# Attention with a gated dense block: head 0 one query tile at a time, its keys transposed on TensorE, wo loaded later

## The chip, the cores, the metric

One core of one Trainium2 chip. The metric is the device time of one execution, in microseconds (us). In the profile lines PE is TensorE, PEld its weight loads, DVE is VectorE, ACT is ScalarE, POOL is GpSimd and SP is SyncE, whose queue issues most of the loads.

## The reference, cut to what matters

```python
xn = _layernorm(x)                                   # x: 2048 x 512
q  = (xn @ wq) -> 32 heads of 128                    # wq: 512 x 4096
scores = einsum(q, k_cache) * 128 ** -0.5            # 2048 keys per head
o  = softmax(scores) @ v_cache                       # per head
s  = o @ wo                                          # wo: 4096 x 512
h  = relu(xn @ w1 + b1) ** 2                         # w1: 512 x 1792
g  = silu(h @ w2 + b2)
return x + s * g
```

## The kernel before: the parts that matter

Queries come in 4 blocks of 512, each with 32 heads: 128 pairs of block and head, called heads 0 to 127. A head has 8 steps of two key tiles (128 keys each); step pi belongs to head pi // 8. In each step TensorE does two score matmuls of 512 columns, up to three *fillers*, and eight PV matmuls for the step two earlier. ScalarE does one exponential of 1024 columns. Fillers are everything else TensorE has to do: later heads' projections, the dense block, wo. PV is the product of the exponentials with the values. In PSUM, psA holds scores, psO the PV sums, psF what fillers make; NPR is 8, LAG is 2.

```python
for pi in range(NPAIR):                      # 1024 steps
    g, k = divmod(pi, NPR)
    gen_scores(pi)                           # waits: exp of pi-2, keys, queries of head g
    ...
    most = 0 if pi == 0 else 4 if pi == 1 else 3 if k == 2 else 2
    while n < most:                          # fillers, paced by a credit (work left / steps left)
        ...
        fill_one(pi)
    if pi >= LAG:
        gen_pv(pi - LAG)                     # waits: exp of pi-2
```

Fillers alternate between two PSUM banks. A job fills one bank with its matmuls, VectorE copies it out, and the job after next needs that bank again:

```python
    (n, mm, evac), i = cur[0]
    bank = bank_no[0]
    mm(i, bank)                              # waits for t_bankF[bank]
    if i == n - 1:
        t_bankF[bank] = evac(bank, step)     # the VectorE copy that frees it
        bank_no[0] ^= 1
```

Head 0 starts cold. Before, all four query tiles of the first block were normalised, transposed and projected; the keys came by a DMA transpose; then the eight steps ran as for any head:

```python
    fill_k(0)                                # DMA transpose, 512 KB
    ...                                      # statistics and scales of 4 tiles
    warm_up(15)                              # dummy matmuls, for the clock
    first_transpose(0); warm_up(3); first_transpose(1); ...
    first_proj(0); first_transpose(2); ...; first_proj(3)
    first_evac(3, 1, DV)
    t_evac[0] = t_bankF[1]                   # the first score waits for this
```

The softmax here doesn't subtract the row's maximum and nothing guards it: scores larger than these inputs give would overflow.

Of the kernel before, what the change touches and what calls it, by code (L numbers as in the profile page):

```python
# [6 lines left out]
ALU = mybir.AluOpType  # L7
# [207 lines left out]
def bass_recurrent_scan__mha_block_cached__dense_activation_squared_relu__prompt_kernel(  # L215
# [84 lines left out]
    psO = nc.alloc_psum_tensor("psO", [P, 2, 2, 256], F32)  # L300
# [4 lines left out]

    sl_k = [S.slot(f"k{i}") for i in range(NSL)]
    sl_v = [S.slot(f"v{i}") for i in range(NSL)]
    sl_wq = [S.slot(f"wq{i}") for i in range(NSW)]
# [34 lines left out]
    def ln_stats(j, i):  # L343
        jt = j * TPB + i
        prev = [t_xn.get(jt - TPB), t_xr.get(jt - TPB)]
        t = E(DV, partial(_bn_stats, out=st_t[:, i, :], in_=x_ln[:, i, :]),
              deps=[t_xl[jt]] + prev)
        t = E(DV, partial(_bn_aggr, out=mv_t[:, i, :], in_=st_t[:, i, :]), deps=[t])
# [4 lines left out]
                                 op=ALU.pow), deps=[t, t_mhalf])  # L353

# [17 lines left out]
    def first_scale(i):  # L372

        t = E(GP, partial(_tt, out=nm_t[:, i:i + 1], in0=mv_t[:, i, 0:1], in1=rstd[:, i:i + 1],
                          op=ALU.mult), deps=[t_xr[i]])
        t = E(GP, partial(_ts, out=nm_t[:, i:i + 1], in0=nm_t[:, i:i + 1], scalar1=-1.0,
                          scalar2=0.0, op0=ALU.mult, op1=ALU.add), deps=[t])
        t_xn[i] = E(AC, partial(_act, out=xn_t[:, i, :], in_=x_ln[:, i, :], func=ACT.Identity,
                                scale=rstd[:, i:i + 1], bias=nm_t[:, i:i + 1]), deps=[t])

    def first_view(i):
        return psA[:, i * 512:i * 512 + 256].bitcast(BF16)

    def first_transpose(i):
        for c in range(NDC):
            t = E(PE, partial(_peT, out=first_view(i)[:, c * P:(c + 1) * P],
                              in_=xn_t[:, i, c * P:(c + 1) * P], ident=ident[:]),
                  deps=[t_xn[i], t_ident], inc=(c == NDC - 1))
        t_xnr[i] = t

    def first_copy(i, eng):
        out, in_ = xnT[:, :, i * P:(i + 1) * P], first_view(i).rearrange("p (c q) -> p c q", q=P)
        op = (partial(_act, out=out, in_=in_, func=ACT.Copy) if eng is AC
              else partial(_copy, out=out, in_=in_))
        tok_xT[0][i] = E(eng, op, deps=[t_xnr[i]])

    def first_proj(i):
        for c in range(NDC):
            t = E(PE, partial(_mm, out=bankF(i // 3)[:, i * P:(i + 1) * P], lhsT=wq_sb[:, 0, c, :],
                              rhs=xnT[:, c, i * P:(i + 1) * P], start=(c == 0),  # L400
                              stop=(c == NDC - 1)),
                  deps=[t_wqfill[0], tok_xT[0][i]], inc=(c == NDC - 1))
        t_proj[0] = t

    def first_evac(i, n, eng):
        out, in_ = qt_sb[:, 0, i * P:(i + n) * P], bankF(i // 3)[:, i * P:(i + n) * P]
        op = (partial(_act, out=out, in_=in_, func=ACT.Copy) if eng is AC
              else partial(_copy, out=out, in_=in_))
        t_bankF[i // 3] = E(eng, op, deps=[t_proj[0]])

    def warm_up(n):
        for _ in range(n):
            E(PE, partial(_mm, out=bankF(1), lhsT=warm[:, 0:P], rhs=warm[:], start=True,
                          stop=True), deps=[t_warm], inc=False)
# [18 lines left out]
    def fill_k(g):  # L433
        if g >= NG:
# [3 lines left out]
                                sl_k[i], deps=[t_S_last[prev] if prev >= 0 else None])  # L438
# [25 lines left out]
    def gen_scores(pi):  # L464
# [4 lines left out]
        for n in range(2):  # L469
            tt = 2 * k + n  # L470
# [343 lines left out]
    for i in range(TPB):  # L814
        ln_stats(0, i)
        if i < 2:
            first_scale(i)
# [124 lines left out]
```

## Time and profile before

| | before |
|---|---|
| time, median of the first 3 runs | 1241.44 us (1240.85 to 1241.76) |
| span in the trace | 1238.3 us |
| TensorE busy / ScalarE busy | 1232.8 / 1057.3 us |
| first score of head 0 starts | 10.75 us |

Busy time of TensorE counts the latency of single matmuls (379 ns on average at 512 columns, though they start 216 ns apart) and the warm-ups, so it says only that there is hardly a gap. Where it works and where it only looks busy has to be read from starts. The prediction shows the lines.

### The profile page before, as it was taken

Reading aid. Unit: us, or ns where it says so; the run is one execution under the profiler, and the core shown is the slowest. Engines: PE = TensorE matmul, PEld = TensorE weight load, DVE = VectorE, ACT = ScalarE, POOL = GpSimd, SP = SyncE. Lnnn points to the kernel's source line nnn. Section 1 sums busy time; section 2 is a strip of 40 time slices with the busy share of each in tenths; the row PEclk is TensorE's granted clock in tenths of the full one; section 3 lists DMA queues with packets and bytes.
Section 4 is the critical chain, followed back from the end, with each engine's and each line's share of the span. In section 5 each row is a group of like instructions: output and inputs, shape, how many; then the busy total and the mean of one; then the engine's idle time right before and its main releaser. Section 6 shows DMA issues by size and latency. Waiting matters only on the chain.

```text
span 1238.3 us, 26720 instructions
## 1 busy us (share of the span) xinstructions
PE 1232.8 (100%) x11793; PEld 813.7 (66%) x11793; DVE 472.4 (38%) x947; ACT 1057.3 (85%) x1048; POOL 32.3 (3%) x74
## 2 busy tenths in 40 slices
PE   9999999999999999999999999999999999999999
PEld 5666666666666666666666666666666666666665
DVE  4452333344434333334443433234444333333333
ACT  7888888888888888888888888888888888888985
POOL 1000000000001000000000100000000010000000
PEclk9999999999999999999999999999999999999999
DMA  9999868877888988788878889777878897877861
GB/s 201 233 216 235 163 132 142 145 137 129 145 161 147 157 147 142 148 133 137 142 146 149 156 155 161 135 134 149 143 130 146 157 156 138 153 139 135 158 126 31
DMA packets 686963, 185.39 MB, mean 150 GB/s; under 512 B 675424, under 2 KB 685920, under 8 KB 686848
## 3 DMA queue, kind: packets, MB, share of 16 engines
q1 hardware_dynamic: 684608, 179.49, 80.4%
q0 software_dynamic: 1424, 3.81, 1.2%
q8 instruction: 93, 1.52, 0.5%
q10 hardware_dynamic: 816, 0.39, 0.1%
q14 instruction: 22, 0.18, 0.1%
HBM read 96.08 MB, written 2.10 MB: 79 GB/s over the span
## 4 chain that ended last, share of the span: by engine, by line
PE 98%; DMA 1%; DVE 0%; ACT 0%; issue 0%; POOL 0%; SPq 0%; DVEq 0%
PE psO L157 37%; PE psA L152 36%; PE psF L152 25%; DMA wq_sb<-in_A_wq_dram 1%; DMA x_ln<-in_A_x_dram 0%; DVE out_t L165 0%; DVE tmp_t L175 0%; PE psA L196 0%; ACT xn_t L161 0%; DVE o_un L179 0%; DVE st_t L200 0%; DVE o_bf L165 0%; ACT xnT L161 0%; POOL rstd L165 0%; DVE qt_sb L179 0%
## 5 line engine op out<-in xcount | busy, mean ns | idle before, releaser
L161 ACT ACTIVATE pT<-psA 128x1024 bf16<-128x1024 f32 x1024 | 1045.4, 1024 | 161.2 <-PE psA L152 116.6
L157 PEld LDWEIGHTS psO<-v_sb,pT 128*128 128x128 bf16 x8192 | 548.1, 98 | 241.5 <-issue 17.0
L157 PE MATMUL psO<-v_sb,pT 128*128 128x129 bf16 x8192 | 631.3, 220 | 0.0
L152 PE MATMUL psA<-qt_sb,kT 128*128 128x512 bf16 x2048 | 609.0, 379 | 0.5 <-DVE qt_sb L179 0.4
L179 DVE COPY o_un<-psO 128x258 f32<-128x258 f32 x256 | 97.2, 421 | 387.7 <-PE psO L157 387.6
L152 PE MATMUL psF<-xnT,wq_sb 128*128 128x512 bf16 (+1 forms) x524 | 167.6, 374 | 0.5 <-DMA wq_sb<-in_A_wq_dram 0.3
L152 PE MATMUL psF<-wo_all,oT 128*128 128x512 bf16 x480 | 164.5, 379 | 0.0
L152 PEld LDWEIGHTS psA<-qt_sb,kT 128*128 128x128 bf16 x2048 | 158.2, 98 | 1.3 <-issue 0.6
L179 DVE CAST qt_sb<-psF 128x512 bf16<-128x512 f32 (+1 forms) x128 | 87.9, 687 | 123.3 <-PE psF L152 123.3
L152 PEld LDWEIGHTS psF<-xnT,wq_sb 128*128 128x128 bf16 x524 | 50.7, 98 | 61.3 <-DMA wq_sb<-in_A_wq_dram 0.9
L165 DVE TENSOR_TENSOR o_bf<-o_un,rden 128x512 bf16<-128x512 f32 x128 | 88.5, 691 | 4.6 <-DVE rden L183 0.3
L152 PEld LDWEIGHTS psF<-wo_all,oT 128*128 128x128 bf16 x480 | 46.9, 98 | 56.4
L171 DVE TENSOR_SCALAR r_t<-psF,b1f 128x512 bf16<-128x512 f32 x56 | 41.9, 748 | 100.2 <-PE psF L152 100.2
L152 PE MATMUL psF<-xnT,w_sb 128*128 128x512 bf16 x224 | 79.7, 379 | 0.0
L152 PE MATMUL psF<-w_sb,h2T 128*128 128x512 bf16 x224 | 73.6, 379 | 0.0
L152 PEld LDWEIGHTS psF<-w_sb,h2T 128*128 128x128 bf16 x224 | 21.9, 98 | 26.4
L152 PEld LDWEIGHTS psF<-xnT,w_sb 128*128 128x128 bf16 x224 | 21.9, 98 | 26.3
L165 DVE TENSOR_TENSOR z_t<-psF,b2bc 128x512 f32<-128x512 f32 x16 | 11.1, 692 | 63.9 <-PE psF L152 63.9
L165 DVE TENSOR_TENSOR acc<-psF,acc 128x512 f32<-128x512 f32 x28 | 19.3, 690 | 35.8 <-PE psF L152 35.8
L208 POOL DMA_DIRECT2D out_dram<-out_t x12 | 6.7, 561 | 870.0 <-DVE out_t L165 870.0
L165 DVE TENSOR_TENSOR h2T<-r_t 128x512 bf16<-128x512 bf16 x56 | 23.8, 425 | 1.9
L183 DVE RECIPROCAL rden<-o_un 128x4 f32<-128x4 f32 x128 | 22.8, 178 | 4.4
(44 smaller groups left out, 152.6 us busy)
## 6 DMA issues: line engine op xcount, KB each, us to landing
v_sb<-in_A_v_cache_dram SPq DMA_DIRECT2D x128, 512.0 KB, 4.8
wq_sb<-in_A_wq_dram SPq DMA_DIRECT2D x127, 128.0 KB, 3.2
wo_all<-in_A_wo_dram SPq DMA_DIRECT2D x4, 1024.0 KB, 6.1
kT<-in_A_k_cache_dram SPq DMA_TRANSPOSE x128, 4.6
oT<-o_bf SPq DMA_TRANSPOSE x128, 4.1
x_t<-in_A_x_dram POOLq DMA_DIRECT2D x16, 128.0 KB, 3.8
x_ln<-in_A_x_dram SPq DMA_DIRECT2D x14, 128.0 KB, 2.9
w_sb<-in_B_w_dram SPq DMA_DIRECT2D x1, 1792.0 KB, 10.6
```

The source lines that it names most:

```text
L152: return e.matmul(out, lhsT, rhs, start=start, stop=stop)
L157: return e.matmul(out, lhsT, rhs, start=start, stop=stop, skip_group_check=True)
L161: return e.activation(out, in_, func, bias=bias, scale=scale)
L165: return e.tensor_tensor(out, in0, in1, op)
L171: return e.tensor_scalar(out, in0, scalar1=scalar1, scalar2=scalar2, op0=op0, op1=op1)
L179: return e.tensor_copy(out, in_)
L183: return e.reciprocal(out, in_)
L208: return e.dma_start(out, in_)
```

## The change

Intent: start the first score as soon as one query tile is ready, not four. For that, a step of head 0 takes one query tile against eight key tiles (still 1024 columns for the exponential), and query tile i+1 is prepared between the steps of tile i. Keys and values of head 0 are loaded as plain halves, the keys transposed on TensorE and copied by ScalarE. With two PSUM banks taken by the preparation, there is no room for fillers in head 0 until step 6. wo is loaded later.

```diff
+    def load_k0(b):                          # plain half of the keys
+    def k0_transpose(b):                     # 8 transposes on TensorE into psO
+    def k0_copy(b):                          # ScalarE: psO -> kT
@@ gen_scores
+        if g == 0:
+            qt, b = divmod(pi, 2)            # query tile, half of the keys
+            for c in range(NKT // 2):        # 8 scores of 128 columns
+                t = E(PE, partial(_mm_shared, ...),
+                      deps=[t_k0[b], t_q0[qt], t_exp[pi - 2] if pi >= 2 else None], ...)
@@ start
-    for i in range(TPB):
-        ln_load(0, i, SP if i % 2 == 0 else AC)
-    fill_k(0)
-    fill_wq(0, AC)
+    ln_load(0, 0, SP)
+    ln_load(0, 1, AC)
+    load_k0(0)
+    fill_wq(0, AC)
+    ln_load(0, 2, SP)
+    ln_load(0, 3, AC)
+    load_k0(1)
@@ ...
-    warm_up(15)
+    warm_up(11)
+    k0_transpose(0)
+    k0_copy(0)
+    ...
+    first_transpose(0)
+    k0_transpose(1)
+    k0_copy(1)
+    first_copy(0)
+    first_proj(0)
@@ wo
-        at(4 * NPR + 6 + 2 * NPR * i, partial(load_wo, i))
+        at(7 * NPR + 3 * NPR * i, partial(load_wo, i))
@@ head 0
+    def first_step(pi):
+        i = pi // 2
+        if pi % 2 == 0:
+            if i:
+                first_proj(i); first_evac(i); ...; gen_pv(pi - 2)
+            gen_scores(pi)
+            if i == TPB - 1:                 # step 6
+                fill_one(pi); fill_one(pi)
+        else:
+            gen_scores(pi)
+            if i < TPB - 1:
+                first_transpose(i + 1); first_copy(i + 1); ...
+            else:                            # step 7
+                fill_one(pi); fill_one(pi)
+            if pi > 1:
+                gen_pv(pi - 2)
@@ main loop
-        most = 0 if pi == 0 else 4 if pi == 1 else 3 if k == 2 else 2
+        most = 0 if pi < NPR else 3 if k == 2 else 2
```

More of the change, by code (lines that the diff above doesn't have):

```diff
@@ L299, in bass_recurrent_scan__mha_block_cached__dense_activation_squared_relu__prompt_kernel @@
     psA = nc.alloc_psum_tensor("psA", [P, 4 * 512], F32)
-    psO = nc.alloc_psum_tensor("psO", [P, 2, 2, 256], F32)
+    psO = nc.alloc_psum_tensor("psO", [P, 2 * 512], F32)
     psF = nc.alloc_psum_tensor("psF", [P, 2 * 512], F32)
@@ L304, in bankF, with bankO @@
         return psF[:, i * 512:(i + 1) * 512]
+    def bankO(i):
+        return psO[:, i * 512:(i + 1) * 512]
     sl_k = [S.slot(f"k{i}") for i in range(NSL)]
     sl_v = [S.slot(f"v{i}") for i in range(NSL)]
+    sl_k0 = [S.slot("k0a"), S.slot("k0b")]
+    sl_v0 = S.slot("v0b")
     sl_wq = [S.slot(f"wq{i}") for i in range(NSW)]
@@ L341, in ln_load, with ln_bn, ln_rstd @@
             deps=[t_xn.get(jt - TPB)])
-    def ln_stats(j, i):
+    t_bn = {}
+    def ln_bn(j, i):
+        jt = j * TPB + i
+        t_bn[jt] = E(DV, partial(_bn_stats, out=st_t[:, i, :], in_=x_ln[:, i, :]),
+                     deps=[t_xl[jt], t_xn.get(jt - TPB), t_xr.get(jt - TPB)])
+    def ln_rstd(j, i):
         jt = j * TPB + i
         prev = [t_xn.get(jt - TPB), t_xr.get(jt - TPB)]
-        t = E(DV, partial(_bn_stats, out=st_t[:, i, :], in_=x_ln[:, i, :]),
-              deps=[t_xl[jt]] + prev)
-        t = E(DV, partial(_bn_aggr, out=mv_t[:, i, :], in_=st_t[:, i, :]), deps=[t])
+        t = E(DV, partial(_bn_aggr, out=mv_t[:, i, :], in_=st_t[:, i, :]), deps=[t_bn[jt]] + prev)
         t = E(DV if j == 0 else GP,
@@ L353, in ln_stats @@
                                  op=ALU.pow), deps=[t, t_mhalf])
+    def ln_stats(j, i):
+        ln_bn(j, i)
+        ln_rstd(j, i)
     def ln_scale(j, i):
@@ L370, in ln_next @@
         ln_transpose(j, i)
-    def first_scale(i):
-        t = E(GP, partial(_tt, out=nm_t[:, i:i + 1], in0=mv_t[:, i, 0:1], in1=rstd[:, i:i + 1],
-                          op=ALU.mult), deps=[t_xr[i]])
-        t = E(GP, partial(_ts, out=nm_t[:, i:i + 1], in0=nm_t[:, i:i + 1], scalar1=-1.0,
-                          scalar2=0.0, op0=ALU.mult, op1=ALU.add), deps=[t])
-        t_xn[i] = E(AC, partial(_act, out=xn_t[:, i, :], in_=x_ln[:, i, :], func=ACT.Identity,
-                                scale=rstd[:, i:i + 1], bias=nm_t[:, i:i + 1]), deps=[t])
@@ L381, in first_view @@
-    def first_view(i):
-        return psA[:, i * 512:i * 512 + 256].bitcast(BF16)
+    t_k0 = [None, None]
+    t_kT0 = [None, None]
+    t_q0 = [None] * TPB
+    t_xT = [None] * TPB
+    def load_k0(b):
+        n = NKT // 2
+        t_k0[b] = S.emit_dma(
+            SP, partial(_dma, out=kT[:, NSL - 1, b * n * P:(b + 1) * n * P],
+                        in_=A_k_cache[0, 0].rearrange("(p t) d -> p (t d)",
+                                                      p=P)[:, b * n * P:(b + 1) * n * P]),
+            sl_k0[b])
@@ new lines, in load_v0 @@
+    def load_v0(b):
+        n = NKT // 2
+        t_v0[b] = S.emit_dma(
+            SP, partial(_dma, out=v_sb[:, 0, b * n:(b + 1) * n, 0:Dh],
+                        in_=A_v_cache[0, 0].rearrange("(p t) d -> p t d",
+                                                      p=P)[:, b * n:(b + 1) * n, :]),
+            [sl_v[0], sl_v0][b])
+    t_v0 = [None, None]
+    def k0_transpose(b):
+        n = NKT // 2
+        for c in range(n):
+            t_kT0[b] = E(PE, partial(_peT, out=bankO(b).bitcast(BF16)[:, c * P:(c + 1) * P],
+                                     in_=kT[:, NSL - 1, (b * n + c) * P:(b * n + c + 1) * P],
+                                     ident=ident[:]),
+                         deps=[t_k0[b], t_ident], inc=(c == n - 1))
@@ L384, in first_transpose @@
+    def k0_copy(b):
+        n = NKT // 2 * P
+        t_k0[b] = E(AC, partial(_act, out=kT[:, 0, b * n:(b + 1) * n],
+                                in_=bankO(b).bitcast(BF16), func=ACT.Copy), deps=[t_kT0[b]])
     def first_transpose(i):
         for c in range(NDC):
-            t = E(PE, partial(_peT, out=first_view(i)[:, c * P:(c + 1) * P],
-                              in_=xn_t[:, i, c * P:(c + 1) * P], ident=ident[:]),
-                  deps=[t_xn[i], t_ident], inc=(c == NDC - 1))
-        t_xnr[i] = t
@@ L391, in first_copy @@
-    def first_copy(i, eng):
-        out, in_ = xnT[:, :, i * P:(i + 1) * P], first_view(i).rearrange("p (c q) -> p c q", q=P)
-        op = (partial(_act, out=out, in_=in_, func=ACT.Copy) if eng is AC
-              else partial(_copy, out=out, in_=in_))
-        tok_xT[0][i] = E(eng, op, deps=[t_xnr[i]])
+            t_xT[i] = E(PE, partial(_peT, out=bankF(1)[:, 0:256].bitcast(BF16)[:, c * P:(c + 1) * P],
+                                    in_=xn_t[:, i, c * P:(c + 1) * P], ident=ident[:]),
+                        deps=[t_xn[i], t_ident, tok_xT[0][i - 1] if i else None],
+                        inc=(c == NDC - 1))
@@ L397, in first_proj, with first_copy @@
+        t_xnr[i] = t_xT[i]
+    def first_copy(i):
+        tok_xT[0][i] = E(
+            DV, partial(_copy, out=xnT[:, :, i * P:(i + 1) * P],
+                        in_=bankF(1)[:, 0:256].bitcast(BF16).rearrange("p (c q) -> p c q", q=P)),
+            deps=[t_xT[i]])
     def first_proj(i):
         for c in range(NDC):
-            t = E(PE, partial(_mm, out=bankF(i // 3)[:, i * P:(i + 1) * P], lhsT=wq_sb[:, 0, c, :],
-                              rhs=xnT[:, c, i * P:(i + 1) * P], start=(c == 0),
-                              stop=(c == NDC - 1)),
-                  deps=[t_wqfill[0], tok_xT[0][i]], inc=(c == NDC - 1))
@@ L403, in first_proj @@
-        t_proj[0] = t
-    def first_evac(i, n, eng):
-        out, in_ = qt_sb[:, 0, i * P:(i + n) * P], bankF(i // 3)[:, i * P:(i + n) * P]
-        op = (partial(_act, out=out, in_=in_, func=ACT.Copy) if eng is AC
-              else partial(_copy, out=out, in_=in_))
-        t_bankF[i // 3] = E(eng, op, deps=[t_proj[0]])
+            t_proj[0] = E(PE, partial(_mm, out=bankF(0)[:, i * P:(i + 1) * P],
+                                      lhsT=wq_sb[:, 0, c, :], rhs=xnT[:, c, i * P:(i + 1) * P],
+                                      start=(c == 0), stop=(c == NDC - 1)),
+                          deps=[t_wqfill[0], tok_xT[0][i], t_q0[i - 1] if i else None],
+                          inc=(c == NDC - 1))
@@ L411, in warm_up, with first_evac @@
+    def first_evac(i):
+        t_q0[i] = E(DV, partial(_copy, out=qt_sb[:, 0, i * P:(i + 1) * P],
+                                in_=bankF(0)[:, i * P:(i + 1) * P]), deps=[t_proj[0]])
     def warm_up(n):
         for _ in range(n):
-            E(PE, partial(_mm, out=bankF(1), lhsT=warm[:, 0:P], rhs=warm[:], start=True,
+            E(PE, partial(_mm, out=psA[:, 0:512], lhsT=warm[:, 0:P], rhs=warm[:], start=True,
                           stop=True), deps=[t_warm], inc=False)
@@ L437, in fill_k @@
         t_kfill[g] = S.emit_dma(SP, partial(_dmaT, out=kT[:, i, :], in_=A_k_cache[0, h, :, :]),
-                                sl_k[i], deps=[t_S_last[prev] if prev >= 0 else None])
+                                sl_k[i], deps=[t_S_last[prev] if prev >= 0 else t_kT0[1]])
     def fill_v(g, eng=SP):
@@ L468, in gen_scores @@
         t = None
-        for n in range(2):
-            tt = 2 * k + n
-            t = E(PE, partial(_mm, out=psA[:, s2 * 1024 + n * 512:s2 * 1024 + (n + 1) * 512],
-                              lhsT=kT[:, i, tt * P:(tt + 1) * P], rhs=qt_sb[:, g % NQS, :],
-                              start=True, stop=True),
-                  deps=[t_exp[pi - 2] if pi >= 2 else None, t_kfill[g], t_evac[g],
-                        t_bankF[0] if pi == 0 else None],
-                  inc=(n == 1))
+        if g == 0:
+            qt, b = divmod(pi, 2)
+            for c in range(NKT // 2):
+                t = E(PE, partial(_mm_shared, out=psA[:, s2 * 1024 + c * P:s2 * 1024 + (c + 1) * P],
+                                  lhsT=kT[:, 0, (b * NKT // 2 + c) * P:(b * NKT // 2 + c + 1) * P],
+                                  rhs=qt_sb[:, 0, qt * P:(qt + 1) * P], start=True, stop=True),
+                      deps=[t_k0[b], t_q0[qt], t_exp[pi - 2] if pi >= 2 else None],
+                      inc=(c == NKT // 2 - 1))
+        else:
+            for n in range(2):
+                tt = 2 * k + n
+                t = E(PE, partial(_mm, out=psA[:, s2 * 1024 + n * 512:s2 * 1024 + (n + 1) * 512],
+                                  lhsT=kT[:, i, tt * P:(tt + 1) * P], rhs=qt_sb[:, g % NQS, :],
+                                  start=True, stop=True),
+                      deps=[t_exp[pi - 2] if pi >= 2 else None, t_kfill[g], t_evac[g],
+                            t_bankF[0] if pi == 0 else None],
+                      inc=(n == 1))
         if k == NPR - 1:
@@ L482, in gen_scores @@
                       deps=[t, t_PV[pi - NPT] if pi >= NPT else None])
+    t_bank = [None, None]
     def gen_pv(pi):
@@ L487, in gen_pv @@
         last = k == NPR - 1
-        order = [(n, qt) for n in range(2) for qt in range(TPB)]
+        if k == 0:
+            t_bank[:] = [None, None]
+        order = [(2 * k + n, qt, n * QB + qt * P) for n in range(2) for qt in range(TPB)]
         if last or k == 0:
-            order = [(n, qt) for b in range(2) for qt in (2 * b, 2 * b + 1) for n in range(2)]
-        t_bank = [None, None]
+            order = [(2 * k + n, qt, n * QB + qt * P) for b in range(2)
+                     for qt in (2 * b, 2 * b + 1) for n in range(2)]
+        if g == 0:
+            order = [(k % 2 * (NKT // 2) + n, k // 2, n * P) for n in range(NKT // 2)]
         t = None
-        for idx, (n, qt) in enumerate(order):
-            tt, b = 2 * k + n, qt // 2
-            tt_first = tt == 0
-            inc = idx == 7 or (last and idx == 3)
-            t = E(PE, partial(_mm_shared, out=psO[:, b, qt % 2, 0:Dh + 1],
-                              lhsT=pT[:, pi % NPT, n * QB + qt * P:n * QB + (qt + 1) * P],
+        for idx, (tt, qt, p0) in enumerate(order):
+            b = qt // 2
+            inc = idx == 7 or (last and g > 0 and idx == 3)
+            t = E(PE, partial(_mm_shared, out=bankO(b)[:, qt % 2 * 256:qt % 2 * 256 + Dh + 1],
+                              lhsT=pT[:, pi % NPT, p0:p0 + P],
                               rhs=v_sb[:, i, tt, 0:Dh + 1],
-                              start=(tt_first and qt % 2 == 0), stop=(tt == NKT - 1)),
-                  deps=[t_exp[pi], t_vfill[g], t_ones,
+                              start=(tt == 0 and qt % 2 == 0), stop=(tt == NKT - 1)),
+                  deps=[t_exp[pi], t_v0[k % 2] if g == 0 else t_vfill[g], t_ones,
                         t_oev[g - 1][b] if g >= 1 else None], inc=inc)
@@ L510, in gen_pv @@
                 t_oev[g][b] = E(DV, partial(_copy, out=o_un[:, s, 2 * b:2 * b + 2, 0:Dh + 1],
-                                            in_=psO[:, b, :, 0:Dh + 1]),
+                                            in_=bankO(b).rearrange("p (s c) -> p s c", s=2)[:, :, 0:Dh + 1]),
                                 deps=[t_bank[b], t_onorm[g - 2] if g >= 2 else None])
@@ L734, in bass_recurrent_scan__mha_block_cached__dense_activation_squared_relu__prompt_kernel @@
     cur = [None]
-    bank_no = [0]
+    bank_no = [1]
     cur_proj = [None]
@@ L798, in load_w1 @@
             sl_w1[i])
-    for i in range(TPB):
-        ln_load(0, i, SP if i % 2 == 0 else AC)
-    fill_k(0)
+    ln_load(0, 0, SP)
+    ln_load(0, 1, AC)
+    load_k0(0)
     fill_wq(0, AC)
+    ln_load(0, 2, SP)
+    ln_load(0, 3, AC)
+    load_k0(1)
     E(AC, partial(_act, out=th_t[:, 0, 0:1], in_=warm[:, 0:1], func=ACT.Exp), deps=[t_warm])
-    fill_v(0)
+    load_v0(0)
+    load_v0(1)
     fill_wq(1)
+    fill_k(1)
     fill_wq(2)
     load_w1(0)
-    fill_k(1)
     fill_v(1)
@@ L813, in bass_recurrent_scan__mha_block_cached__dense_activation_squared_relu__prompt_kernel, with load_b1, load_b2 @@
     at(8, partial(load_w1, 3))
-    for i in range(TPB):
-        ln_stats(0, i)
-        if i < 2:
-            first_scale(i)
-    warm_up(15)
-    first_transpose(0)
-    warm_up(3)
-    first_transpose(1)
-    first_copy(0, AC)
-    first_copy(1, AC)
-    ln_scale(0, 2)
-    ln_scale(0, 3)
-    warm_up(2)
-    first_proj(0)
-    first_transpose(2)
-    first_copy(2, AC)
-    first_proj(1)
-    first_transpose(3)
-    first_copy(3, DV)
-    first_proj(2)
-    first_evac(0, 3, AC)
-    first_proj(3)
-    first_evac(3, 1, DV)
-    t_evac[0] = t_bankF[1]
-    tok_b1 = S.emit_dma(GP, partial(_dma, out=b1b[:], in_=B_b1.rearrange("(c p) -> c p", p=P)),
-                        sl_b1)
-    tok_b2 = S.emit_dma(GP, partial(_dma, out=b2bc[:],
-                                    in_=bass.AP(tensor=B_b2.tensor, offset=B_b2.offset,
-                                                ap=[[0, P], [1, D]])), sl_b2)
+    warm_up(11)
+    k0_transpose(0)
+    k0_copy(0)
+    ln_bn(0, 0)
+    ln_rstd(0, 0)
+    ln_bn(0, 1)
+    ln_scale(0, 0)
+    first_transpose(0)
+    k0_transpose(1)
+    k0_copy(1)
+    t_kfill[0] = t_k0[1]
+    ln_rstd(0, 1)
+    first_copy(0)
+    first_proj(0)
+    warm_up(1)
+    first_evac(0)
+    ln_scale(0, 1)
+    ln_bn(0, 2)
+    t_evac[0] = t_q0[0]
+    tok_b1 = tok_b2 = None
+    def load_b1():
+        nonlocal tok_b1
+        tok_b1 = S.emit_dma(GP, partial(_dma, out=b1b[:],
+                                        in_=B_b1.rearrange("(c p) -> c p", p=P)), sl_b1)
+    def load_b2():
+        nonlocal tok_b2
+        tok_b2 = S.emit_dma(GP, partial(_dma, out=b2bc[:],
+                                        in_=bass.AP(tensor=B_b2.tensor, offset=B_b2.offset,
+                                                    ap=[[0, P], [1, D]])), sl_b2)
+    at(2 * NPR, load_b2)
     tok_w2 = None
@@ L859, in bass_recurrent_scan__mha_block_cached__dense_activation_squared_relu__prompt_kernel @@
         at(j * SPB + SPB // 2, partial(load_xt, j))
+    def first_step(pi):
+        i = pi // 2
+        if pi % 2 == 0:
+            if i:
+                first_proj(i)
+                first_evac(i)
+                if i < TPB - 1:
+                    ln_scale(0, i + 1)
+                if i < TPB - 2:
+                    ln_bn(0, i + 2)
+                gen_pv(pi - 2)
+            gen_scores(pi)
+            if i == TPB - 1:
+                t_bankF[:] = [t_q0[i], tok_xT[0][i]]
+                fill_one(pi)
+                fill_one(pi)
+        else:
+            gen_scores(pi)
+            if pi == 5:
+                load_b1()
+            if i < TPB - 1:
+                first_transpose(i + 1)
+                first_copy(i + 1)
+                if i < TPB - 2:
+                    ln_rstd(0, i + 2)
+            else:
+                fill_one(pi)
+                fill_one(pi)
+            if pi > 1:
+                gen_pv(pi - 2)
     left = [sum(job[0] for _, _, job, _ in jobs) + n_in]
@@ L865, in bass_recurrent_scan__mha_block_cached__dense_activation_squared_relu__prompt_kernel @@
         g, k = divmod(pi, NPR)
-        gen_scores(pi)
+        if pi < NPR:
+            first_step(pi)
+        else:
+            gen_scores(pi)
         credit = min(credit + left[0] / max(end - pi, 1), 8.0)
         n = 0
-        most = 0 if pi == 0 else 4 if pi == 1 else 3 if k == 2 else 2
+        most = 0 if pi < NPR else 3 if k == 2 else 2
         while n < most:
@@ L883, in bass_recurrent_scan__mha_block_cached__dense_activation_squared_relu__prompt_kernel @@
             print(pi, n, round(credit, 1), jobs[0][0] if jobs else None, len(pending))
-        if pi >= LAG:
+        if pi >= NPR:
             gen_pv(pi - LAG)
```

## The prediction

> **What bounds the kernel now.** I read the page first (busy shares, the chain that ended last, the costliest groups), then the waits of TensorE, then the first 12 us of the chain, then TensorE's own timeline where head 0 ends and where the run ends.
>
> ```profile
> PE 1232.8 (100%) x11793; PEld 813.7 (66%) x11793; DVE 472.4 (38%) x947; ACT 1057.3 (85%) x1048; POOL 32.3 (3%) x74
> ...
> PE 98%; DMA 1%; DVE 0%; ACT 0%; issue 0%; POOL 0%; SPq 0%; DVEq 0%
> PE psO L157 37%; PE psA L152 36%; PE psF L152 25%; DMA wq_sb<-in_A_wq_dram 1%; DMA x_ln<-in_A_x_dram 0%; DVE out_t L165 0%; DVE tmp_t L175 0%; PE psA L196 0%; ACT xn_t L161 0%; DVE o_un L179 0%; DVE st_t L200 0%; DVE o_bf L165 0%; ACT xnT L161 0%; POOL rstd L165 0%; DVE qt_sb L179 0%
> ...
> L161 ACT ACTIVATE pT<-psA 128x1024 bf16<-128x1024 f32 x1024 | 1045.4, 1024 | 161.2 <-PE psA L152 116.6
> ```
>
> TensorE is 98% of the chain. Its waits, in order of size (columns: engine, line, releaser; total us, times, longest), come to 2.4 us in 1238, and only the fourth lies outside the first 11 us:
>
> ```profile
> PE psF L152 <- DVE warm L187: 1.2, 1, 1.2
> PE psA L152 <- DVE qt_sb L179: 0.4, 1, 0.4
> PE psA L196 <- ACT xn_t L161: 0.3, 1, 0.3
> PE psF L152 <- DMA wq_sb<-in_A_wq_dram: 0.3, 1, 0.3
> ```
>
> So what can be won is time in which TensorE does nothing needed. Most lies before the first score. The chain there (start, duration, what):
>
> ```profile
> 0.72 2.67 DMA x_ln<-in_A_x_dram
> ...
> 3.42 0.70 DVE st_t L200
> ...
> 4.61 0.58 POOL rstd L165
> ...
> 5.75 0.82 ACT xn_t L161
> ...
> 9.00 0.61 ACT xnT L161
> ...
> 9.65 0.69 PE psF L152 x8
> ...
> 10.36 0.30 DVE qt_sb L179
> ...
> 10.75 1.02 PE psA L152 x4
> ```
>
> The first score waits for all four query tiles to be normalised, transposed and projected, and starts at 10.75. TensorE looks 8.57 us busy up to there, but that is mostly 20 warm-up matmuls; needed are 16 transposes and 16 projections of 128 columns, 32 x 0.056 = 1.8 us. About 9.0 us are empty or dummy, and that is nearly all the change can reach. Then the steady rate, from TensorE's timeline at the end of head 0:
>
> ```profile
> 20.59 0.59 PE L152 MATMUL psA<-qt_sb,kT 128*128 128x512 bf16 x2
> 21.02 0.38 PE L152 MATMUL psF<-xnT,w_sb 128*128 128x512 bf16 x1
> 21.23 0.62 PE L157 MATMUL psO<-v_sb,pT 128*128 128x129 bf16 x8
> 21.69 0.59 PE L152 MATMUL psA<-qt_sb,kT 128*128 128x512 bf16 x2
> ```
>
> The starts are what counts, since durations overlap: two scores 0.43, one filler matmul 0.21 (fillers are the projections, the dense block and wo, slipped in between), eight PV matmuls 0.46. A step with one filler takes 1.10 us, with two 1.32, with none 0.89. The exponentials, in a run without a gap near the end, take 23.90/23 = 1.04 each:
>
> ```profile
> 1199.84 23.90 ACT L161 ACTIVATE pT<-psA 128x1024 bf16<-128x1024 f32 x23 [0.23 <-PE psA L152]
> ```
>
> So a step with a filler is TensorE's and one without is ScalarE's (it loses up to 0.15). Step 8, the first of head 1, starts at 21.69.
>
> **What the Trainium skill says.** "TensorE: Matmul & The Clock Gate", section "Back-to-back issue gap", gives N/2.4 + 2.5 ns as the gap of single matmuls (216 at 512 columns, 56 at 128) and says streams with weight loads differ (about 81 at 128); the trace has 216 and 56 with weight loads in the stream, so the split of two 512-column scores into eight 128-column ones should cost about 8 x 0.056 - 0.43 = 0.02 us, not more. The same page, Part 4 "PE-mode transpose", says a transpose comes at 275 to 390 ns and does not count as activity for the clock; here four take 0.40 from first start to last end, so they pipeline like matmuls. Whether they hold the clock the trace does not separate. The same page, Part 1, puts the full clock at about 3.4 us of sustained activity: here the warm-ups go from 0.43 to 0.22 us each at 4.6 us, 3.4 us after the first. "DMA: Bandwidth & Descriptors", section "Anatomy of one DMA", has a fixed part of about 2 us (for GpSimd's path): the first 128 KB of x take 2.67 here, so a plainly loaded key half cannot be ready at once either.
>
> **The change, part by part.**
>
> *Start of the first score.* The order of instructions shows: DVE does statistics of tile 0 (3.42 to 4.15), aggregate and ve (to 4.53), POOL the root (4.61 to 5.19), then DVE scales (the row in the trace: 0.40, so to about 5.7), without POOL's two nm instructions and with 0.40 in place of ScalarE's 0.82. Eleven warm-ups end near 5.3; eight key transposes (0.45) overlap that. The four transposes of tile 0 end near 6.2, then the second eight key transposes (0.45, to 6.7), the xnT copy on DVE (0.42, to 6.8), projection (4 x 0.056, to 7.2 with the pipeline), qt copy (0.29, after some 0.2 of hand-over, to 7.7). First score at about 7.8, instead of 10.75. The key copies on ScalarE, each estimated at an exponential's 1.02 for the same 1024 columns, run 5.9 to 7.9. A risk is the second key half: x, k and wq up to there are 1.15 MB, and the trace moves 230 to 370 GB/s in this stretch, so it lands between 6 and 7 us; and it stands before the first projection on TensorE. I add 0.1: first score 7.9.
>
> *Head 0.* Per query tile (two steps) TensorE has 16 scores (0.90), 16 PV (0.91), 4 transposes and 4 projections (0.45): 2.26. ScalarE has 2 x 1.04 = 2.08. Not hidden: the copy of xnT (0.2 + 0.42 + 0.07 against one PV of 0.45: 0.24) and of qt (0.2 + 0.29 + 0.09 against 0.45: 0.13). So 2.6 a tile, three tiles 7.8, score 6 at 15.7. Steps 6 and 7 carry two fillers each: 0.45 + 0.43 + 0.45 + 0.43 + 0.46 = 2.2. Step 8 starts at 17.9: 3.8 earlier than 21.69.
>
> *Work put off.* Counted in the order of instructions, before does 15 fillers in steps 0 to 7, after 4. The 11 left over are done later at 0.216: 2.4 us. By step 1000 both have done 1400.
>
> *The end.* The put-off work does not spread evenly: after has 17 steps without filler in the last 64, before 12, among them two runs of four. In before the pattern is mostly one filler, one, none: 1.10 + 1.10 + 0.89 = 3.09 against 3 x 1.04 = 3.12, so nothing is lost. A run of four without filler loses two or so times 0.15 after TensorE's lead is used up. Two runs: 0.6 us back.
>
> *DMA.* One DMA transpose of 512 KB (3.19 us in SP's queue) becomes two plain loads, so SP's queue runs 2 to 3 us earlier; TensorE at step 32 is also earlier, by about 3.8 - 6 x 0.216 = 2.5. The one wait on wq (the gap is 0.45 by the starts, 48.95 to 49.83 less 0.43) belongs to a projection that moves one step later, so I expect it gone: -0.4. wo is needed from step 78 at the earliest and issued at 56, 80, 104, 128 instead of 38, 54, 70, 86; no wait of TensorE lies there now, so it gains nothing.
>
> Sum: -3.8 + 2.4 + 0.6 - 0.4 = -1.2 us. 1241.44 - 1.2 = 1240.2.
>
> **The rivals.** (1) The 3 us at the start arrive whole: 1238. Against it: TensorE is the bound, and fillers not done in head 0 are done elsewhere; for it, only if the later steps had idle TensorE, which the waits deny. (2) Head 0 hangs on the DVE round (scale, copy, projection, copy) more than reckoned, each hand-over 0.2 longer, about 0.5 a tile: step 8 at 20, result 1242. For it: DVE also has statistics of 0.68 in this round and is strictly in order. Against: in before the same kinds followed each other with 0.02 to 0.09. (3) The clock falls back in head 0, since transposes and gaps stand where dense matmuls stood: a window of 3.4 us at half speed costs about 1.7 us, result 1242. Against: before also has gaps of 0.2 to 0.4 here and stayed fast. (4) The DMA queues, full up to 70 us (SP has no pause in the trace there), cannot follow a head that ends 3.8 us earlier; the wq wait grows to 1 to 2 us: 1242. Against: one heavy transfer fewer ahead of them.
>
> **Range and chances.** The gain is a difference of terms about 3 us in size, each good to 0.7, so 1238.4 to 1242.2. A 2% change would be 25 us; nothing touched is that large. Faster 0.005, same 0.985, slower 0.01.
>
> **What would show it.** Right: first score near 7.9 and step 8 (first 512-column score) near 17.9; no wait on wq near 49; 0.3 to 0.8 us of new idle TensorE in the last 60 steps. Wrong: step 8 after 19 with gaps on qt or xnT copies (rival 2), matmul starts 0.43 apart at 512 columns after 5 us (rival 3), new waits on wq, keys or values between 20 and 70 us (rival 4), or an end 3 us earlier (rival 1).

## The result, and the profile after

| | before | after |
|---|---|---|
| median of 6 runs | 1240.91 us | 1242.52 us |
| lowest, highest | 1240.15, 1241.76 | 1242.40, 1243.62 |
| span in the trace | 1238.3 us | 1240.7 us |
| first score of head 0 | 10.75 us | 8.47 us |
| first score of head 1 (step 8) | 20.59 us | 19.04 us |
| fillers in steps 0 to 7 | 15 | 4 |

A ratio here is the mean time of one kernel's fast runs over the mean of the other's of the same rounds, so not quite the ratio of the medians quoted. It is 1.0015 (95% interval 1.0002 to 1.0028): a small loss, within the class of 2%, where a small gain was predicted, and outside the predicted range of 1238.4 to 1242.2.

The page of the changed kernel still has TensorE on nearly all of the chain (some matmul records are missing in this trace, so its busy sum is not compared):

```profile
PE 97%; issue 1%; DVE 1%; DMA 0%; ACT 0%; SPq 0%; ACTq 0%; DVEq 0%
```

Its waits are new ones (engine, line, what was waited for; total us, times, longest):

```profile
PE psF L152 <- DVE b1f L179: 1.4, 1, 1.4
...
PE psF L152 <- DVE xnT L179: 0.5, 1, 0.5
PE psA L152 <- DVE qt_sb L179: 0.4, 1, 0.4
...
PE psO L196 <- DMA kT<-in_A_k_cache_dram: 0.2, 1, 0.2
```

The wait on wq of before is gone, and a wait of 1.4 us, once, now heads the list. The chain of the changed kernel, in order of time, shows where the waits stand. First its start (start, duration, what):

```profile
2.11 4.99 DMA kT<-in_A_k_cache_dram
7.15 0.62 PE psO L196 x8
7.77 0.24 PE psF L152 x4
8.03 0.30 DVE qt_sb L179
...
8.47 1.05 PE psA L157 x16
```

The second key half, issued at 2.11, lands at 7.10. Its transposes stand before the first projection in TensorE's order, so the chain runs through it. It is the last of two gates by little: the projection starts at 7.61, and the copy of xnT that it also needs, late because TensorE's clock rose late in this run, ends at 7.45. Then the seam between heads 0 and 1:

```profile
17.74 0.45 PE psF L152 x2
18.20 0.70 DVE qt_sb L179
...
19.04 0.59 PE psA L152 x2
...
21.66 0.44 DVE o_un L179
22.12 0.19 DVE rden L183
22.33 0.69 DVE o_bf L165
23.02 0.60 DVE qt_sb L179
23.62 0.09 DVE b1f L179
23.77 0.38 PE psF L152
```

Two times the chain leaves TensorE for VectorE. Step 8 waits for head 1's queries, whose last projection matmul is only done in step 7. And from 21.66 to 23.77 the chain runs on VectorE, which works off head 0's output (o_un, rden, o_bf), then casts head 2's queries (copies them to bf16), then copies b1. TensorE meanwhile does one filler and the b1 transpose, and then stands still. By the starts, the filler at 21.89 and the b1 transpose would let the next filler start near 22.17; it starts at 23.77, 1.6 us late.

The list of waits names b1f as the releaser. By the program it is the cast before it: b1's job has the one bank, and the projection of head 3 needs the other one, which is free when head 2's queries are cast. The times allow it: the cast ends at 23.62, TensorE's weight load starts at 23.74, and from cast to weight load the other such waits in head 0 and step 8 take 0.06 to 0.12.

One more reading is needed before the sum. TensorE's own timeline of the kernel before, only the score matmuls, from the first one on:

```profile
10.75 1.02 PE L152 MATMUL psA<-qt_sb,kT 128*128 128x512 bf16 x4 [0.43 <-DVE qt_sb L179]
...
12.46 0.60 PE L152 MATMUL psA<-qt_sb,kT 128*128 128x512 bf16 x2
...
14.00 0.59 PE L152 MATMUL psA<-qt_sb,kT 128*128 128x512 bf16 x2
...
15.32 0.59 PE L152 MATMUL psA<-qt_sb,kT 128*128 128x512 bf16 x2
...
16.64 0.59 PE L152 MATMUL psA<-qt_sb,kT 128*128 128x512 bf16 x2
...
17.95 0.59 PE L152 MATMUL psA<-qt_sb,kT 128*128 128x512 bf16 x2
...
19.27 0.59 PE L152 MATMUL psA<-qt_sb,kT 128*128 128x512 bf16 x2
```

The first row has x4: it holds steps 0 and 1. Counting on, 19.27 is step 7 and the row at 20.59 in the prediction is step 8. The prediction counted rows, and took 21.69, which is step 9.

### The profile page after: what moved, and what is told of

Read it like the earlier page. It is cut to its first block, busy times and chain, and to the rows that moved or that the text cites. A ratio compares the mean times of both kernels' runs of the same rounds, so it can differ in the third digit from the quotient of the medians.

```text
span 1240.7 us, 26627 instructions
## 1 busy us (share of the span) xinstructions
PE 1222.4 (99%) x11641; PEld 816.5 (66%) x11849; DVE 474.1 (38%) x955; ACT 1053.6 (85%) x1044; POOL 31.5 (3%) x70
## 4 chain that ended last, share of the span: by engine, by line
PE 97%; issue 1%; DVE 1%; DMA 0%; ACT 0%; SPq 0%; ACTq 0%; DVEq 0%
PE psO L157 37%; PE psA L152 35%; PE psF L152 25%; DMA kT<-in_A_k_cache_dram 0%; PE psA L157 0%; ACT pT L161 0%; DVE qt_sb L179 0%; DVE out_t L165 0%; DVE xnT L179 0%; SPq L208 0%; DVE tmp_t L175 0%; ACTq L134 0%; PE psF L196 0%; DVE o_bf L165 0%; PE psO L196 0%
## 5 line engine op out<-in xcount | busy, mean ns | idle before, releaser
L152 PE MATMUL psA<-qt_sb,kT 128*128 128x512 bf16 x1843 | 563.6, 379 | 10.3 <-DVE qt_sb L179 0.4
L152 PE MATMUL psF<-xnT,wq_sb 128*128 128x512 bf16 (+1 forms) x510 | 163.2, 374 | 2.4 <-DVE b1f L179 1.4
```

What stands on the lines that cost most here:

```text
L152: return e.matmul(out, lhsT, rhs, start=start, stop=stop)
```

## The experiments

Kernels of one session ran on the same chip as fresh runs of the kernel before; medians are given with those of before in the same session. All results were correct. Times of step starts and gaps are from the traces.

**1. b1 after head 3's projection.** The suspected wait at step 10, taken away by moving what uses up the bank's turn.

```diff
-    jobs = [(3, 3, job_b1(), None)]
+    jobs = [(9.5, 3, job_b1(), None)]
```

> The changed kernel with one edit: the transpose of b1 is taken after the projection of head 3 instead of before it. My theory: the 1.6 us gap of TensorE at step 10 (23.8 us) is a wait of the next projection for its PSUM bank; the tiny b1 job uses up the other bank's turn, so the bank is still held by the cast of head 2's queries, which stands on VectorE behind head 0's output copies. Then the gap at step 10 falls under 0.2 us, at most 0.6 us comes back where b1 now stands, and the time falls by 1.0 to 1.6 us, to about 1241.2. Rival: VectorE is simply late at the end of head 0 and would hold TensorE with or without b1; then the gap stays over 1 us and the time stays within 0.4 us of 1242.5.

Measured: 1241.10 us (before: 1240.67), ratio 1.0004 (0.9991 to 1.0017). TensorE's timeline of this kernel at the same place:

```profile
21.51 0.59 PE L152 MATMUL psA<-qt_sb,kT 128*128 128x512 bf16 x2
21.94 0.81 PE L152 MATMUL psF<-xnT,wq_sb 128*128 128x512 bf16 x3
22.59 0.62 PE L157 MATMUL psO<-v_sb,pT 128*128 128x129 bf16 x8
```

Three fillers run without a pause where the changed kernel stood still. VectorE has the same work at the same time (the cast of head 2's queries starts at 22.99, in the changed kernel at 22.94), so the rival falls: VectorE was late, but nothing had to wait for it. Where b1 now stands, 0.16 us are lost, as in the kernel before at its step 4. I timed it again in another session:

> The one-line edit b1_later timed again beside it: if the wait on the filler's bank is what makes the changed kernel slower than before, it is again within 0.5 us of the kernel before and 1.0 to 1.6 us under 1242.5; rival: the first timing was favoured by its chip, and it comes out at 1242 or more.

1240.98 us (before: 1240.24), ratio 1.0007 (0.9995 to 1.0020). Its medians, 1.4 and 1.5 us under the changed kernel's 1242.52, come from other sessions; the ratios to before fall from 1.0015 to 1.0004 and 1.0007, which is 1.0 to 1.4 us.

**2. Head 1's projection wholly in step 6.**

```diff
             if i == TPB - 1:
                 t_bankF[:] = [t_q0[i], tok_xT[0][i]]
                 fill_one(pi)
                 fill_one(pi)
+                fill_one(pi)
+                fill_one(pi)
@@ step 7
-            else:
-                fill_one(pi)
-                fill_one(pi)
```

> The changed kernel with one edit: all four matmuls of head 1's projection are done in step 6 rather than two each in steps 6 and 7. My theory: step 8 waits some 0.6 us for the cast of these queries, which can only start after the last of the four; done earlier, the cast lies beside step 7 and its PV, and step 8 starts 0.4 to 0.5 us earlier (about 18.55 us instead of 19.01), time about 1242.0. Rival: step 8 also needs exponential 6 and TensorE has the same work to do, so nothing moves: step 8 at 19.0, 1242.5.

Measured: 1242.16 us (before: 1240.67), ratio 1.0013 (1.0000 to 1.0026). From first score to step 8 it takes 10.12 us instead of 10.57, so the wait shrank by 0.45 as expected. The absolute start of step 8, expected at 18.55, was later instead (19.45): in this trace the second key half landed at 8.0, and the first score started at 9.33. The timed difference to the changed kernel, about 0.3 us and from two sessions, is too small to stand by itself.

**3. Both edits.**

> The two edits together. If the two waits are separate, the gains add: 1.4 to 2.1 us off, about 1240.8, level with the kernel before. If the second only moves into the first (TensorE then reaches the busy stretch of VectorE earlier), the gain is that of the larger one alone, about 1241.2.

Measured: 1240.68 us (before: 1240.67), ratio 1.0001 (0.9988 to 1.0013). In the same session it is 0.4 us under experiment 1 and 1.5 us under experiment 2: the gains add. With the two waits out, the changed kernel is level with the kernel before.

**4. The old head, with wo loaded later.** This part of the change alone.

> The kernel before with only the later loads of wo. My theory: wo is needed from step 78 on and no wait of TensorE lies where its loads stood, so nothing: within 0.3 us of the kernel before (1240.9), wq wait at step 32 still 0.3 to 0.5 us. Rival: the loads of wo crowd the queue and the wq wait at step 32 goes (0.4 us faster), or later loads make a new wait.

Measured: 1241.49 us (before: 1240.67), ratio 1.0006 (0.9992 to 1.0020). No gain. Its five runs spread over 1.5 us and overlap those of before, so no loss is shown either. The wq wait at step 32 is there, larger by its starts (0.84 us; before 0.46). wo's first load comes at step 38 or later in both kernels, so wo cannot be the cause: the wq load in question landed at 50.4 us here and at 49.8 before, and TensorE wants it at about 49.4 in the trace of before. This wait varies between traces of the same opening. My bound of 0.3 us for the timed difference was too tight.

**5. The old head with few fillers.** The put-off work alone: the kernel before, but only 4 fillers in head 0.

```diff
-        most = 0 if pi == 0 else 4 if pi == 1 else 3 if k == 2 else 2
+        most = (2 if pi in (4, 5) else 0) if pi < NPR else 3 if k == 2 else 2
```

(and b1 placed as in experiment 1)

> The kernel before, its old head 0 untouched, but with only 4 fillers in steps 0 to 7 (head 1's projection, in steps 4 and 5) instead of 15, and b1's transpose after head 3's projection. It tests the put-off term alone. My theory: a filler left out of head 0 is paid later at 0.216 us, so step 8 starts 1.7 to 2.2 us earlier (about 18.6 us instead of 20.5), and the end does not gain: 0.2 to 0.7 us slower than before, because steps without a filler are ScalarE's (1.04 instead of 0.89). Rival: an earlier step 8 is an earlier end, 1.5 to 2 us faster than before.

Measured: 1240.95 us (before: 1240.79), ratio 1.0002 (0.9990 to 1.0015). TensorE's timeline:

```profile
18.76 0.59 PE L152 MATMUL psA<-qt_sb,kT 128*128 128x512 bf16 x2
```

This is step 8: 1.83 us earlier than before, with a start of the first score no earlier at all, and the last step starts 0.16 us later than before. An early step 8 is no gain by itself. The 11 fillers left out cost 11 x 0.216 = 2.4 us later on; the wq wait happened to be absent in this trace, which hides 0.46. So the first half of the theory was met; the loss at the end, 0.16 us in time and trace, is just under the 0.2 to 0.7 expected and, in time, within the noise.

**6. The second key half before x tiles 2 and 3.** On top of experiment 3.

```diff
-    ln_load(0, 2, SP)
-    ln_load(0, 3, AC)
     load_k0(1)
+    ln_load(0, 2, SP)
+    ln_load(0, 3, SP)
```

> The changed kernel with both waits taken out (edits of both_waits), and the loads of x tiles 2 and 3 put behind the second key half. My theory: the first score waits for the second key half (its transposes stand before the first projection on TensorE), which shares the DMA queues with two x tiles that nobody needs yet; then it lands 0.5 to 0.8 us earlier, the first score starts near 8.0 instead of 8.5 to 9.3 us, and the time falls by about 0.4 us to 1240.3. Rival: the first score is set by the late clock of TensorE or by the VectorE chain, and the time stays at 1240.7.

Measured: 1240.29 us (before: 1240.79), ratio 0.9995 (0.9982 to 1.0009). TensorE's wait for the keys is gone from the list of waits. The second half was issued at 1.65 instead of 2.11 and was 4.4 us under way instead of 5.0, so it landed at 6.01 instead of 7.10; in the six traces with the old order of loads it takes 4.9 to 5.8, which fits loads in each other's way. But the first score in the profiled run was no earlier (8.62): the warm-ups and the first key transposes ran at half speed, and the copy of xnT came late. Both of my readings hold in part: several gates stand there, and a trace shows only the last. The timed difference, 0.4 us to a kernel of another session, is not settled.

How the clock moves between runs is seen in the eleven warm-up matmuls, the same in all these kernels. In the changed kernel's trace:

```profile
1.18 4.88 PE L152 MATMUL psA<-warm 128*128 128x512 bf16 x11 [1.18 <-DVE warm L187]
5.84 0.93 PE L196 MATMUL psO<-ident,kT 128*128 128x128 bf16 x8
```

and in that of experiment 1's kernel:

```profile
1.18 4.18 PE L152 MATMUL psA<-warm 128*128 128x512 bf16 x11 [1.18 <-DVE warm L187]
...
7.21 0.62 PE L196 MATMUL psO<-ident,kT 128*128 128x128 bf16 x8 [1.03 <-DMA kT<-in_A_k_cache_dram]
```

With 4.88 all eleven started 0.43 us apart (the first pair 0.40), and the first key transposes still 0.11 apart instead of 0.056. With 4.18 the clock had risen before the end. By these spacings it rose 3.4 us after the first warm-up in experiment 1's trace and in that of before, as the prediction reckoned, but only 5.3 us after it in the changed kernel's. Nothing was won by the early rise: the second key half came no earlier (7.16), and alone held the first score to 8.52, against 8.47. A second trace of the unedited changed kernel was taken to see what varies:

> The changed kernel again, unedited, for a second trace. If the late rise of TensorE's clock (6.5 us in the first trace, 4.5 and 5.4 us in two edited ones) and the landing of the second key half vary from run to run, the first score again lies anywhere between 8.0 and 9.3 us; if they belong to the kernel, it starts at 8.4 to 8.5 with the clock rising at 6.5.

One run of 1242.83 us (alone, so its state is unknown; the granted clock is 1.0). Warm-ups 4.60, key half waited for (1.0 us, to 7.48), first score at 8.80, and every gap in head 0 and at step 10 again the same within 0.01 us. So the opening moves by some 0.3 us between these two, and what the program sets does not; over the six traces with this opening the first score starts anywhere from 8.34 to 9.33.

**7. Each query tile one tile ahead.** On top of experiment 6: tile 1 is transposed before step 0 and projected inside it, tile 2 in steps 2 and 3, tile 3 in steps 4 and 5, each behind scores that can already run. b1 is loaded at the start and transposed in step 1, outside the alternation of banks. This frees the banks in step 5, so 6 fillers fit in head 0.

```diff
+        gen_scores(pi)
+        if pi == 0:
+            first_proj(1); ln_bn(0, 2); first_evac(1); ln_rstd(0, 2); ln_bn(0, 3)
+        elif pi == 1:
+            (b1: transpose into the free half bank, copy on VectorE)
+            ln_scale(0, 2); ln_rstd(0, 3)
+        elif pi == 2:
+            gen_pv(0); first_transpose(2); first_copy(2); ln_scale(0, 3)
+        elif pi == 3:
+            first_proj(2); first_evac(2); gen_pv(1)
+        elif pi == 4:
+            first_transpose(3); first_copy(3); gen_pv(2)
+        elif pi == 5:
+            first_proj(3); first_evac(3); (2 fillers); gen_pv(3)
+        else:
+            (2 fillers); gen_pv(pi - 2)
```

> keys_first, and in addition each query tile is transposed and projected one tile earlier, between scores that can already run, so that copies on VectorE lie beside scores and PV; b1 is loaded at the start and transposed in step 1. My theory: the 0.8 + 0.4 + 0.4 us of idle TensorE in head 0 go, 6 fillers instead of 4 fit in, step 8 starts near 16.7 us, and the time is 1 to 2 us under both kernels, about 1239. Rival: VectorE, strictly in order, is full in head 0 (statistics, scale and two copies per tile are about 2 us against 2.1 us of two exponentials), so the gaps only move: step 8 after 18 us, time over 1240.

Measured: 1239.39 us (before: 1240.79), ratio 0.9989 (0.9976 to 1.0001). Timed again:

> The same kernel as tile_ahead, timed again, since its interval against the kernel before (0.9976 to 1.0001) just touches 1. If it is truly faster, the ratio is again 0.9985 to 0.9992; if that was chance, it is within 0.0003 of 1.

1239.10 us (before: 1240.24), ratio 0.9991 (0.9977 to 1.0005). In each of the two sessions all five runs are under all nine runs of before, by 1.4 and 1.1 us at the median, though each interval contains 1. Against experiment 6, in the same session, all five runs are faster too (1238.94 to 1239.70 against 1239.76 to 1240.81). It is the fastest version; which of its parts brings how much was not tried. TensorE's waits in the second trace, without that before the warm-ups:

```profile
PE psA L157 <- ACT pT L161: 0.3, 1, 0.3
PE psO L157 <- ACT pT L161: 0.3, 1, 0.3
PE psA L157 <- DVE qt_sb L179: 0.2, 1, 0.2
PE psF L152 <- DVE xnT L179: 0.2, 1, 0.2
```

Two of the four waits are now ScalarE's. Step 8 starts at 18.2 and 17.9 us in the two traces, with two more fillers done. I had expected 16.7: about 1.1 us of idle TensorE remain in steps 0 to 7 (2.1 in the changed kernel; both are the time between the starts less 0.056 us for each matmul of 128 columns and 0.216 for each of 512), partly still behind VectorE's copies. My theory was right in direction and too large; the rival's "after 18 us" was met in one of the two traces, but not its time.

## Why the prediction was wrong

Two steps carry most of the miss: the row taken for step 8, which made the gain of head 0 look 1.10 us larger than it could be, and a wait of 1.6 us at step 10, for which the prediction had no term. A later first score (0.57) and the wait of step 8 (0.6) add the rest. The sum of the prediction and what the traces show for each term, in us (negative is faster):

| term | predicted | measured or counted |
|---|---|---|
| start of step 8 against before | -3.8 | 19.04 - 20.59 = -1.55 |
| 11 fillers put off | +2.4 | 11 x 0.216 = +2.4 |
| wait for a bank at step 10 | 0 | +1.6 |
| wq wait at step 32 | -0.4 | -0.45 |
| end of the run | +0.6 | +0.3 |
| sum | -1.2 | +2.3 |

The last scores of the run start 2.3 us later than before and the spans differ by 2.4, so the table closes. It compares two traces; the timed medians differ by only 1.6. The traced run of before took 1240.14 us, 0.8 under the median of its six, that of the changed kernel 1242.47, at its median. The +0.3 at the end is 0.07 of more idle time and one filler more done before the last step (0.22).

**The frame was right.** TensorE is the bound, little of the change reaches the end, work left out of head 0 is paid later at 0.216 us apiece. Experiment 5 shows it; besides the fillers it changes only b1's place. So was "within 2%", given 0.985.

**The first step that failed is "Step 8, the first of head 1, starts at 21.69".** It is 20.59, and the trace of before had it. A row of a merged timeline can hold two steps; rows were counted in place of matmuls. That is 1.10 us of the 2.25 that the first term is off, and alone moves the prediction from 1240.2 to 1241.3. The old head 0 was not 10.94 us long but 9.84, with 15 fillers in it: there was less to win than the prediction thought.

**"First score 7.9" was 8.47**, another 0.57. The second key half was named as a risk and given 0.1. It landed at 7.10, just beyond the 6 to 7 us of the text. In this trace it accounts for only 0.1: without it the projection could have started at about 7.5 instead of 7.61, after the copy of xnT. The rest is the clock, which the prediction took to rise as in the trace of before: the key transposes began at 5.84, not beside warm-ups that end near 5.3, and ran at the low clock, so tile 0's transposes began at 6.61. Experiment 6 removes the first gate and meets the second; experiment 1's trace, with the early clock, shows the first alone.

**"2.6 a tile" held**: the first scores of the tiles start at 8.47, 11.05, 13.64 and 16.24, which is 2.6 each. For the first tile that is chance, as TensorE's timeline of the changed kernel shows:

```profile
8.47 1.05 PE L157 MATMUL psA<-qt_sb,kT 128*128 128x128 bf16 x16 [0.26 <-DVE qt_sb L179]
9.36 0.39 PE L196 MATMUL psF<-ident,xn_t 128*128 128x128 bf16 x4
10.27 0.40 PE L152 MATMUL psF<-xnT,wq_sb 128*128 128x128 bf16 x4 [0.52 <-DVE xnT L179]
10.50 0.62 PE L157 MATMUL psO<-v_sb,pT 128*128 128x129 bf16 x8
11.05 1.07 PE L157 MATMUL psA<-qt_sb,kT 128*128 128x128 bf16 x16
```

The prediction gave every tile 16 PV matmuls; this round has eight, 0.45 us less, and nothing lies beside the copy of xnT, so the gap before the projection is 0.69 by the starts instead of 0.24. The two errors cancel. In the next two rounds both terms are as predicted.

**"Step 8 starts at 17.9" missed a wait.** Steps 6 and 7 took 2.80 instead of 2.2. The prediction put two fillers in each of these steps and forgot what they were: the projection whose cast step 8 needs. Experiment 2 takes 0.45 of the 0.6 back. With the 1.10 and the 0.57 this is the 2.25.

**No term for step 10.** The prediction listed four rivals, one of them a busy VectorE, but looked for it within head 0. The wait came two steps after it, from the order of the filler jobs: with fewer fillers in head 0, b1's one-matmul job falls into the stretch in which VectorE copies out head 0. Experiment 1 shows that b1's place in the order is what makes it cost: 1.6 us in the trace, 1.0 to 1.4 in time.

**"-0.4, I expect it gone"** came true, in all nine traces with the new head 0. The same wait was 0.46, 0.84 and absent in the traces of three kernels with the old head (in the third with other fillers ahead of it). The reason given, SP's queue running earlier, fits the traces: this load of wq was issued at 43.4 to 43.8 and landed at 49.7 to 50.4 in those three, at the edge of the need; in the changed kernel's trace it was issued at 40.8 and landed at 46.1. But TensorE was not 2.5 us earlier at step 32, as the prediction had it: it was 1.4 later, which alone makes the load less urgent.

**wo** gains nothing, as said; experiment 4 shows none. **"0.6 us back"** at the end was oversized: 0.07 of idle time. The runs of four steps without filler are short, and the exponentials of the changed kernel ran at 21.44/21 = 1.02 us there, not 1.04.

**The rivals.** Rival 1 (3 us arrive whole) did not occur; that a put-off filler is paid later, the argument against it, is shown by experiment 5. Rival 2 gave the right time, 1242, for the wrong place, which is luck: the round took 2.6 as reckoned. Rival 3 (the clock falls back) did not occur: head 0's matmuls keep the full-speed spacing (16 scores from 8.47 to 9.36, 0.056 each). Rival 4 (the DMA queues cannot follow) did not occur: no new wait on wq, keys or values between 20 and 70 us.

Open: how much the loading of keys as plain halves costs or gains by itself was not tried alone. In the trace of before the transposed keys landed at 1.65 + 5.6 = 7.2 us (7.8 to 7.9 in the other two traces with the old head), in the changed kernel the plain halves at 5.2 and 7.1. But these can be used only once ScalarE has copied them from PSUM, at 7.8 and 8.8, so in these traces the keys were ready no earlier than before, and the second half about 1 us later. Why the second half lands anywhere from 7.0 to 8.0 in traces of the same opening is also open.

## What to carry to other kernels

When one engine is the bound all along, an earlier start is worth only the idle time it removes: count the work that moves out of the opening as a debt, and pay it in the sum. When jobs alternate between two buffers, a tiny job takes a whole turn, and the next but one then waits for a copy that had no time to be made: keep tiny jobs out of the alternation. Count instructions, not rows, when a timeline merges them.

## What the Trainium skill lacked or had wrong

- "TensorE: Matmul & The Clock Gate", section "Back-to-back issue gap": the sustained figures for streams of weight load and matmul (about 81 ns at 128 columns, 131 at 512) do not fit. The starts give 0.45/8 = 56 ns at 128 to 129 columns and 216 ns at 512, weight loads included: the page's figures for single matmuls.
- The same page, Part 4 "PE-mode transpose", gives 275 to 390 ns per transpose and no figure for a series. Here eight of 128 x 128 take 0.62 us from first start to last end once the clock is up, so they follow each other like matmuls of that width (eight PV matmuls take 0.62 too); begun at the low clock, 0.93.
- No page compares a DMA transpose with a plain load followed by transposes on TensorE by the time at which the operand can be used, the copy out of PSUM included: here 7.2 us for the DMA transpose, 7.8 and 8.8 us for the two plain halves (landed at 5.2 and 7.1).
